# Splitting the first loads over two queues and moving two small loads back, at the head of a one-core attention and feed-forward kernel

## The chip, the cores and the metric

The kernel runs on one core of one Trainium2 chip. The metric is the device time of one execution in microseconds (us). One profiled execution of each kernel gives a trace; its span is about 1.7 us shorter than the device time. All times "at" a point are us from the span's start.

Engines: PE multiplies matrices, ACT and DVE work elementwise, POOL makes masks, SP only issues DMAs. ACT and POOL issue DMAs too, each on its own queue. POOL's queue is the software one (q0 in the profile), SP's and ACT's are hardware ones (q1 and q10).

## The reference

Two blocks of the same input x (2048 tokens, 512 features, bf16) are mixed by a gate for each token:

```python
g = sigmoid((x * gate_w).sum(-1, keepdims=True))
a = attention(x, wq, wk, wv, wo, beta)   # 32 heads of 16, in 4 segments of 512 tokens,
                                         # with a memory carried from segment to segment
b = ((relu(x @ W_gate)) * (x @ W_up)) @ W_down      # inner width 1792
return g * a + (1 - g) * b
```

Only the loads matter below: x (2 MB), wq, wk, wv (512 KB each), W_gate and W_up (1.8 MB each), and two tiny ones, beta (64 bytes, copied to all 128 partitions: the tile `betab`) and gate_w (1 KB, fetched as 512 separate 2-byte elements: the tile `gw`).

## The kernel before

The whole kernel is planned in Python: a list scheduler fixes the order of every engine's instructions beforehand. The chip then runs these fixed orders with semaphore waits. These are the loads at the head, in order of issue:

```python
    nc.gpsimd.dma_start(out=betab[:], in_=A_beta.partition_broadcast(P))
    with nc.allow_non_contiguous_dma(reason="1 KB"):
        nc.gpsimd.dma_start(out=gw[:], in_=gate_w.rearrange("(c p) -> p c", p=P))
    got_x0 = load(nc.sync, x0[:], x[0:L, :].rearrange("(t p) d -> p t d", p=P), L * D * 2)
    got_q = [load_cols(nc.scalar, wq_sb, A_wq, 0, D)] * 2
    got_k = [load_cols(nc.sync, wk_sb, A_wk, 0, D)] * 2
    got_v = load_cols(nc.scalar, wv_sb, A_wv, 0, D)
    # ... (cut) SP goes on: W_gate and W_up piece 0, then piece 1, then the transposing
    #     load of the second segment of x, then the other pieces, W_down, wo, more of x
```

`nc.sync` is SP, `nc.scalar` ACT, `nc.gpsimd` POOL. While these loads run, PE multiplies zeros to raise its clock; then it transposes segment 0 of x (x0), projects q, k and v, and goes on:

```python
    junk = sb([P, L], BF16, "junk")
    nc.vector.memset(junk[:], 0.0)          # after some other small memsets of DVE
    # ... (cut)
    for k in range(9):
        nc.tensor.matmul(wb[3][:], lhsT=junk[:, 0:P], rhs=junk[:], start=True, stop=True)
    order = plan.run()
    for t in order:
        if t.emit is not None:
            t.emit()
```

The softmax here doesn't subtract the row's maximum and nothing guards it: scores larger than these inputs give would overflow.

## Time and profile before

The time is 292.23 us (median of 3 runs, 292.07 to 292.28).

| What | Value | Where it is read |
|---|---|---|
| PE busy | 282.2 of 290.4 us, 97% | engine table |
| chain that ended last | 90% PE; largest single piece that is not PE: the DMA of wk | chain of waits |
| x0 landed, wq landed | 6.0 and 6.5 us | DMA issues: issue 0.81 plus 5.2 and 5.7 |
| q projections end, first wk matmul | 9.9 and 10.62 us | timeline |
| first large exponential | 14.47 us | timeline |

The piece of the chain of waits (start, length, what):

```profile
1.31 9.26 DMA wk_sb<-in_A_wk_dram
```

Four lines of the timeline (start, length, engine, line, operation, output and inputs, and in brackets how long the engine sat idle before and what ended that):

```profile
6.10 0.61 PE L315 MATMUL wb_133<-ident,E_83 128*128 128x128 bf16 x4 [0.22 <-DMA E_83<-in_A_x_dram]
...
8.88 1.02 PE L300 MATMUL wb_132<-xT,wq_sb 128*128 128x512 bf16 x4
10.62 1.04 PE L300 MATMUL wb_131<-xT,wk_sb 128*128 128x512 bf16 x4 [0.71 <-DMA wk_sb<-in_A_wk_dram]
...
14.47 1.88 ACT L455 ACTIVATE E_76<-sp 128x2048 bf16<-128x2048 f32 x1 [1.34 <-PE sp L434]
```

PE finished q and then waited 0.71 us for wk. From there on it is nearly always busy, so whatever makes wk land sooner moves everything.

Why wk took 9.26 us is in the windows view (busy time and instruction count of PE, PEld (PE's weight loads), DVE, ACT, POOL; the last three columns are PE's granted clock, the mean busy share of the DMA engines, and GB/s). Two columns need care. The clock column shows 1.00 wherever the trace has no record, and the first record here begins at 7.87 us. The DMA share counts every packet from its start to its end, so it exceeds 1 where packets overlap:

```profile
5.00:6.00 1.00, 0.88 (x3) 0.00 (x0) 0.00 (x0) 0.00 (x0) 1.00 (x2) 1.00 1.30 359
6.00:7.00 1.00, 0.90 (x9) 0.90 (x10) 0.25 (x1) 0.00 (x0) 0.44 (x2) 1.00 0.92 81
7.00:8.00 1.00, 1.00 (x11) 0.93 (x9) 0.57 (x2) 0.59 (x1) 0.00 (x0) 1.00 0.86 267
8.00:9.00 1.00, 0.97 (x5) 0.39 (x4) 0.03 (x1) 0.59 (x1) 0.00 (x0) 1.00 1.08 335
```

In 6 to 7 us the DMA engines are still busy for a share of 0.92, but move only 81 GB/s. The view of the DMA queues for 5 to 9 us says what held them (packets, MB, share of 16 engines' time):

```profile
q10 hardware_dynamic: 538, 0.53, 39.6%
q1 hardware_dynamic: 499, 0.50, 37.0%
q0 software_dynamic: 62, 0.01, 27.3%
```

The 62 packets of betab and gw took 27.3% of four microseconds of all sixteen engines, so 1.09 us of each engine, for 0.01 MB.

### The profile page before, as it was taken

Reading aid. Unit: us, or ns where it says so; the run is one execution under the profiler, and the core shown is the slowest. Engines: PE = TensorE matmul, PEld = TensorE weight load, DVE = VectorE, ACT = ScalarE, POOL = GpSimd, SP = SyncE. Lnnn points to the kernel's source line nnn. Section 1 sums busy time; section 2 is a strip of 40 time slices with the busy share of each in tenths; the row PEclk is TensorE's granted clock in tenths of the full one; section 3 lists DMA queues with packets and bytes.
Section 4 is the critical chain, followed back from the end, with each engine's and each line's share of the span. In section 5 each row is a group of like instructions: output and inputs, shape, how many; then the busy total and the mean of one; then the engine's idle time right before and its main releaser. Section 6 shows DMA issues by size and latency. Waiting matters only on the chain.

```text
span 290.4 us, 6923 instructions
## 1 busy us (share of the span) xinstructions
PE 282.2 (97%) x2905; PEld 138.5 (48%) x2905; DVE 176.5 (61%) x442; ACT 194.6 (67%) x168; POOL 88.5 (30%) x141
## 2 busy tenths in 40 slices
PE   7899999999999999999999999999999999999995
PEld 3344545454545353545353545346634545544442
DVE  1599896675946168569692558657947434554211
ACT  1289797789966678879866678787796767433100
POOL 7014443333242424342423243422324243200000
PEclk9999999999999999999999999999999999999999
DMA  6999962010110201100103010000100110010011
GB/s 178 341 277 344 187 121 43 2 21 18 29 29 21 56 18 20 20 18 2 36 2 76 20 36 3 19 2 2 20 18 3 36 38 27 12 20 0 0 36 36
DMA packets 32558, 15.91 MB, mean 55 GB/s; under 512 B 22016, under 2 KB 32528, under 8 KB 32528
## 3 DMA queue, kind: packets, MB, share of 16 engines
q1 hardware_dynamic: 31408, 14.42, 20.5%
q10 hardware_dynamic: 1056, 1.05, 1.1%
q8 instruction: 22, 0.36, 0.5%
q0 software_dynamic: 64, 0.01, 0.4%
q14 instruction: 8, 0.07, 0.1%
HBM read 8.14 MB, written 2.10 MB: 35 GB/s over the span
## 4 chain that ended last, share of the span: by engine, by line
PE 90%; ACT 3%; DMA 3%; DVE 1%; issue 0%; POOL 0%; SPq 0%; ACTq 0%
PE wb_131 L300 24%; PE wb_130 L300 21%; PE wb_133 L300 13%; PE wb_132 L300 10%; PE sp L434 9%; PE wb_132 L482 7%; DMA wk_sb<-in_A_wk_dram 3%; PE wb_130 L482 2%; PE wb_133 L482 1%; PE wb_133 L473 1%; ACT E_79 L455 1%; ACT E_78 L455 1%; ACT E_77 L455 1%; ACT E_76 L455 1%; PE wb_132 L542 1%; PE wb_133 L542 1%
## 5 line engine op out<-in xcount | busy, mean ns | idle before, releaser
L300 PEld LDWEIGHTS <-wu_sb 128*128 128x128 bf16 x224 | 20.2, 98 | 26.3 <-issue 4.9
L300 PEld LDWEIGHTS <-wg_sb 128*128 128x128 bf16 x224 | 19.9, 98 | 24.8 <-issue 4.5
L455 ACT ACTIVATE E_78<-sp 128x2048 bf16<-128x2048 f32 x10 | 18.8, 1877 | 7.0 <-PE sp L434 6.2
L300 PE MATMUL wb_130<-xT,wg_sb 128*128 128x512 bf16 x88 | 23.2, 380 | 0.0
L455 ACT ACTIVATE E_83<-sp 128x2048 bf16<-128x2048 f32 x10 | 18.8, 1876 | 6.3 <-PE sp L434 6.1
L455 ACT ACTIVATE E_79<-sp 128x2048 bf16<-128x2048 f32 x10 | 18.8, 1876 | 6.0 <-PE sp L434 6.0
L455 ACT ACTIVATE E_76<-sp 128x2048 bf16<-128x2048 f32 x10 | 18.8, 1877 | 5.5 <-PE sp L434 5.1
L455 ACT ACTIVATE E_82<-sp 128x2048 bf16<-128x2048 f32 x10 | 18.8, 1875 | 5.5 <-PE sp L434 4.5
L455 ACT ACTIVATE E_77<-sp 128x2048 bf16<-128x2048 f32 x10 | 18.8, 1876 | 5.4 <-PE sp L434 3.3
L455 ACT ACTIVATE E_80<-sp 128x2048 bf16<-128x2048 f32 x10 | 18.8, 1876 | 4.8 <-PE sp L434 4.0
L455 ACT ACTIVATE E_81<-sp 128x2048 bf16<-128x2048 f32 x10 | 18.8, 1876 | 4.2 <-PE sp L434 4.1
L300 PE MATMUL wb_133<-xT,wu_sb 128*128 128x512 bf16 x72 | 18.9, 380 | 0.0
L300 PE MATMUL wb_131<-xT,wu_sb 128*128 128x512 bf16 x72 | 18.7, 380 | 0.0
L461 POOL TENSOR_SCALAR_AFFINE_SELECT E_76<-E_76 128x512 bf16<-128x512 bf16 x16 | 10.3, 661 | 26.1 <-ACT E_76 L455 26.1
L461 POOL TENSOR_SCALAR_AFFINE_SELECT E_81<-E_81 128x512 bf16<-128x512 bf16 x16 | 11.7, 747 | 18.4 <-ACT E_81 L455 18.4
L461 POOL TENSOR_SCALAR_AFFINE_SELECT E_80<-E_80 128x512 bf16<-128x512 bf16 x16 | 10.9, 696 | 18.4 <-ACT E_80 L455 18.4
L461 POOL TENSOR_SCALAR_AFFINE_SELECT E_79<-E_79 128x512 bf16<-128x512 bf16 x16 | 10.2, 651 | 20.1 <-ACT E_79 L455 20.1
L461 POOL TENSOR_SCALAR_AFFINE_SELECT E_83<-E_83 128x512 bf16<-128x512 bf16 x16 | 10.0, 640 | 20.5 <-ACT E_83 L455 20.5
L461 POOL TENSOR_SCALAR_AFFINE_SELECT E_77<-E_77 128x512 bf16<-128x512 bf16 x16 | 10.3, 662 | 18.7 <-ACT E_77 L455 18.7
L461 POOL TENSOR_SCALAR_AFFINE_SELECT E_78<-E_78 128x512 bf16<-128x512 bf16 x16 | 9.9, 637 | 19.6 <-ACT E_78 L455 19.6
L461 POOL TENSOR_SCALAR_AFFINE_SELECT E_82<-E_82 128x512 bf16<-128x512 bf16 x16 | 10.0, 639 | 18.9 <-ACT E_82 L455 18.9
L576 ACT ACTIVATE rg<-wb_130 128x512 bf16<-128x512 f32 x22 | 13.1, 594 | 3.5 <-PE wb_130 L300 3.4
(541 smaller groups left out, 832.8 us busy)
## 6 DMA issues: line engine op xcount, KB each, us to landing
out_dram<-osb SPq DMA_DIRECT2D x16, 128.0 KB, 1.7
wd_sb<-in_B_W_down_dram SPq DMA_DIRECT2D x2, 896.0 KB, 10.4
wg_sb<-in_B_W_gate_dram SPq DMA_DIRECT2D x2, 512.0 KB, 11.5
wu_sb<-in_B_W_up_dram SPq DMA_DIRECT2D x2, 512.0 KB, 11.4
wg_sb<-in_B_W_gate_dram SPq DMA_DIRECT2D x2, 384.0 KB, 5.3
wu_sb<-in_B_W_up_dram SPq DMA_DIRECT2D x2, 384.0 KB, 6.6
wq_sb<-in_A_wq_dram ACTq DMA_DIRECT2D x1, 512.0 KB, 5.7
E_83<-in_A_x_dram SPq DMA_DIRECT2D x1, 512.0 KB, 5.2
```

The costliest lines, as they stand in the source:

```text
L300: nc.tensor.matmul(bank(sl), lhsT=lhsT, rhs=rhs, start=(start and q == 0), stop=(stop and q == n - 1))
L434: nc.tensor.matmul(sp[:, j, off:off + n], lhsT=kt[32 * j:32 * j + 32, kb * P:(kb + 1) * P], rhs=QT[i][32 * j:32 * j + 32, kb * P:kb * P + ...
L455: b = plan.add("ACT", 1880, key, lambda Ef=Ef: nc.scalar.activation(Ef[:], sp[:], ACT.Exp, scale=SCALE), [a] + eread.get(n - RE, []), ACL)
L461: nc.gpsimd.affine_select(out=m, in_=m, compare_op=ALU.is_ge, fill=0.0, base=0, pattern=[[0, 4], [1, P]], channel_multiplier=-1)
L473: nc.tensor.matmul(wb[sl.banks[1]][:, q2 * 136:(q2 + 1) * 136], lhsT=pqT[u % RQ][:, qb * P:(qb + 1) * P], rhs=mbd[i][:, c], start=(q2 == 0 ...
L482: nc.tensor.matmul(bank(sl)[:, lo:lo + HW], lhsT=E[(5 * u + f) % RE][:, j, o:o + P], rhs=Vp[i][:, kb, 8 * c + h8, 0:HW], start=(q2 == 0 an ...
L542: nc.tensor.matmul(wb[sl.banks[g // 2]][:, lo:lo + 136], lhsT=pK[i][:, t, g * P:(g + 1) * P], rhs=Vp[i][:, t, 8 * g:8 * g + 8, 0:HW], star ...
L576: nc.scalar.activation(rg[0][:], bank(sl), ACT.Relu)
```

## The change

The intent: x0 arrives sooner if both queues carry it first; the small loads get out of the way of the projection weights; PE's clock is warm when x0 arrives.

```diff
-    nc.gpsimd.dma_start(out=betab[:], in_=A_beta.partition_broadcast(P))
-    with nc.allow_non_contiguous_dma(reason="1 KB"):
-        nc.gpsimd.dma_start(out=gw[:], in_=gate_w.rearrange("(c p) -> p c", p=P))
-    got_x0 = load(nc.sync, x0[:], x[0:L, :].rearrange("(t p) d -> p t d", p=P), L * D * 2)
-    got_q = [load_cols(nc.scalar, wq_sb, A_wq, 0, D)] * 2
+    def load_halves(dst, src, k, nbytes):
+        src = src.rearrange("(c p) n -> p c n", p=P)
+        nc.sync.dma_start(out=dst[:, 0:k // 2], in_=src[:, 0:k // 2])
+        nc.scalar.dma_start(out=dst[:, k // 2:k], in_=src[:, k // 2:k])
+        return arrival(nbytes)
+
+    got_x0 = load_halves(x0, x[0:L, :], 4, L * D * 2)
+    got_q = [load_halves(wq_sb, A_wq, NC, D * D * 2)] * 2
     got_k = [load_cols(nc.sync, wk_sb, A_wk, 0, D)] * 2
     got_v = load_cols(nc.scalar, wv_sb, A_wv, 0, D)
+    nc.scalar.dma_start(out=betab[:], in_=A_beta.partition_broadcast(P))
+    with nc.allow_non_contiguous_dma(reason="1 KB"):
+        nc.scalar.dma_start(out=gw[:], in_=gate_w.rearrange("(c p) -> p c", p=P))
# ... (cut) the memset of junk moves ahead of DVE's and POOL's other memsets
-    for k in range(9):
+    for k in range(10):
         nc.tensor.matmul(wb[3][:], lhsT=junk[:, 0:P], rhs=junk[:], start=True, stop=True)
```

A constant of the scheduler also went from 3500 to 3300.

More of the change, by code (lines that the diff above doesn't have):

```diff
@@ L169 @@
     x0 = E[RE - 1]
-    clock = [3500.0]
+    clock = [3300.0]
     plan = Plan(4)
@@ L218 @@
     got_x[3] = [load_xT(3)]
+    junk = sb([P, L], BF16, "junk")
+    nc.vector.memset(junk[:], 0.0)
     ident = sb([P, P], BF16, "ident")
@@ L253 @@
     got_gates = plan.add("DVE", 900, 0.0, head_gates, [got_eb], 100)
-    junk = sb([P, L], BF16, "junk")
-    nc.vector.memset(junk[:], 0.0)
     sp = psum.tile([P, 4, L], F32, name="sp")
```

## The prediction

> **What bounds the kernel now.** The engine table gives PE 282.2 us busy of a 290.4 us span (97%), and the chain of waits is PE for 90%. Its one large piece that is not compute is at the head: the DMA of wk, issued at 1.31 us and landed 9.26 us later (3.2%). After it PE runs almost without a gap in a fixed order, so the question is when wk lets PE go on: by the timeline PE ends the second q projection near 9.9 us and waits until 10.62 us for wk. wv lands at 11.4 us and is used at 11.9 us.
>
> **Why wk lands so late.** The windows view shows the DMA rate: 387 and 359 GB/s in 4 to 6 us, then 81 in 6 to 7 us and 267 in 7 to 8 us, then about 346. The dip coincides with the software queue's packets: in 5 to 7 us the view of the DMA queues gives it 48% of all 16 engines for 19 packets and 0.01 MB. These are betab and gw, issued by POOL at 1.32 and 2.01 us and landing 7.0 and 7.9 us later. Against 350 GB/s the dip loses 0.35 MB, or 1.0 us, ahead of wk and wv.
>
> **The change.**
> 1. x0 and wq in halves. Today they land nearly together, at 6.0 and 6.5 us, because two queues share one rate (Trainium skill, "DMA: Bandwidth & Descriptors", section "Issuing engines are not separate DMA queues"; this trace agrees: 292 and 298 packets in 3 to 5 us). In halves x0 gets both shares: it is moved when 512 KB in all are, near 4.6 us by the windows, so landed near 4.9 us. wq stays near 6.3 us. The bytes ahead of wk do not change.
> 2. Small loads behind wv on ACT's queue. They leave the road in front of wk and wv: about 1.0 us, which is the gain. wk lands near 9.6 us, wv near 10.4 us. ACT issues five DMAs of about 0.5 us instead of two, so its table load ends near 4.9 us instead of 3.2, still before the first copy. betab lands near 11.5 to 12 us; its use moves to about 11.9 us, with a microsecond of slack before the first large exponential.
> 3. Ten matmuls on zeros from about 1.25 us instead of nine from 1.86. At 427 ns each they end near 5.5 us, sooner if the clock rises: transposes start there instead of at 6.10 us, and q ends near 9.0 us. This is hidden, as wk comes later.
>
> The order of the remaining instructions on every engine is unchanged.
>
> **On the critical path.** Only wk's landing: 10.57 to about 9.6 us. All that follows shifts whole by about 1.0 us: 291.2 us, with 290.5 to 291.9 us to hold it 8 times in 10. Chances: faster by over 2% 0.01, within 2% 0.98, slower 0.01.
>
> **What the profile would show.** Right: no dip at 6 to 8 us and no software queue; x0 landed by about 5 us, transposes near 5.5 us; the first wk matmul at 9.5 to 9.8 us, still released by the wk DMA; the first large exponential near 13.5 instead of 14.47 us, and the same 1 us at every later point. Wrong: the dip moves rather than disappears, or q instead of the wk DMA releases the wk matmuls.
>
> **What would make it wrong.** The small loads, issued in hardware, cost more engine time than now or slow wv; ACT stalls while issuing them and holds the xT copies; betab lands so late that it delays the first exponentials; or a later wait absorbs the microsecond.

## The result, and the profile after

The changed kernel takes 290.89 us (median of 4 runs, 290.83 to 290.92) against 292.25 us (4 runs) for the kernel before, 1.36 us less. The ratio is 0.9953, with a 95% interval from 0.9936 to 0.9970. Ratios are the mean time of one kernel's fast runs over that of the other's fast runs of the same rounds, so not quite the ratio of the medians quoted.

The piece of the chain of waits, after:

```profile
1.81 7.54 DMA wk_sb<-in_A_wk_dram
```

The timeline, after:

```profile
5.50 0.63 PE L321 MATMUL wb_135<-ident,E_83 128*128 128x128 bf16 x4
...
7.84 1.02 PE L306 MATMUL wb_134<-xT,wq_sb 128*128 128x512 bf16 x4
9.40 1.04 PE L306 MATMUL wb_133<-xT,wk_sb 128*128 128x512 bf16 x4 [0.54 <-DMA wk_sb<-in_A_wk_dram]
...
13.25 1.88 ACT L461 ACTIVATE E_76<-sp 128x2048 bf16<-128x2048 f32 x1 [1.34 <-PE sp L440]
```

wk lands at 9.35 us (1.81 + 7.54) instead of 10.57 us. Its first matmul is 1.22 us sooner, the first large exponential is 1.22 us sooner, and the last scaling of a result tile (DVE, 286.88 us before, 285.68 us after) is 1.20 us sooner. So the whole gain is made before 9.4 us and then carried to the end.

The windows view, after (columns as above):

```profile
6.00:7.00 1.00, 1.00 (x15) 0.84 (x13) 0.70 (x2) 0.63 (x3) 0.00 (x0) 1.00 0.98 313
7.00:8.00 1.00, 0.99 (x5) 0.38 (x4) 0.15 (x1) 0.57 (x2) 0.00 (x0) 1.00 1.07 368
8.00:9.00 1.00, 0.86 (x4) 0.19 (x2) 0.72 (x2) 0.00 (x0) 0.00 (x0) 1.00 1.06 358
9.00:10.00 1.00, 0.60 (x3) 0.31 (x4) 0.67 (x1) 0.00 (x0) 0.00 (x0) 1.00 0.53 154
10.00:11.00 1.00, 1.00 (x7) 0.47 (x5) 0.52 (x1) 0.00 (x0) 0.00 (x0) 1.00 0.95 280
```

The dip at 6 to 8 us is gone. A smaller one stands at 9 to 11 us, where the small loads now run. wk has landed by then, and nothing on the chain waits for what comes next.

One thing was not foreseen. ACT's fifth load (gw) was not issued at about 2.9 us: ACT waited until 4.4 us and issued it by 4.8 us, and the table load behind it ended at 6.13 us. From the timeline:

```profile
2.37 0.55 ACTq L203 DMA_DIRECT2D betab<-in_A_beta_dram  x1
...
4.44 0.38 ACTq L205 DMA_DIRECT2D gw<-in_gate_w_dram  x1
...
4.85 1.28 ACT L326 ACT_TABLE_LOAD   x1 [4.85 <-DMA E_83<-in_A_x_dram]
```

The last bracket names the cause: ACT waited for a half of x0 to land. The semaphores in the trace say why. The program counts the landings on both hardware queues with eight semaphores (counters that a load raises as it lands). From the ninth load on, each load first waits for the landing of the earlier load whose semaphore it takes over. gw took that of ACT's half of x0 (landed at 4.42 us), and SP's next piece of W_up that of the other half (landed at 4.09 us, piece issued at 4.11 us). So this wait belongs to the program, and every extra load on a hardware queue, a half or a small one, brings it sooner.

It did no harm here: ACT's first copy of transposed x started at 6.50 us, just as its input was ready.

### The profile page after: what moved, and what is told of

The parts are those of the page before. It is cut to its first block, busy times and chain, and to the rows that moved or that the text cites. A ratio compares the mean times of both kernels' runs of the same rounds, so it can differ in the third digit from the quotient of the medians.

```text
span 289.2 us, 6881 instructions
## 1 busy us (share of the span) xinstructions
PE 277.7 (96%) x2860; PEld 138.3 (48%) x2906; DVE 176.5 (61%) x442; ACT 194.5 (67%) x168; POOL 87.3 (30%) x139
## 4 chain that ended last, share of the span: by engine, by line
PE 88%; ACT 3%; DMA 3%; issue 2%; another core or an unknown queue 1%; DVE 1%; SPq 0%; POOL 0%; ACTq 0%
PE wb_133 L306 24%; PE wb_132 L306 20%; PE wb_135 L306 13%; PE sp L440 9%; PE wb_134 L306 8%; PE wb_134 L488 7%; DMA wk_sb<-in_A_wk_dram 3%; PE wb_132 L488 2%; PE wb_135 L488 1%; PE wb_135 L479 1%; ACT E_78 L461 1%; ACT E_76 L461 1%; ACT E_79 L461 1%; ACT E_77 L461 1%
## 5 line engine op out<-in xcount | busy, mean ns | idle before, releaser
L306 PE MATMUL wb_135<-xT,wu_sb 128*128 128x512 bf16 x68 | 18.5, 380 | 0.3 <-issue 0.2
L306 PE MATMUL wb_133<-xT,wu_sb 128*128 128x512 bf16 x68 | 18.5, 380 | 0.2
L467 POOL TENSOR_SCALAR_AFFINE_SELECT E_81<-E_81 128x512 bf16<-128x512 bf16 x16 | 11.7, 750 | 18.4 <-ACT E_81 L461 18.4
L467 POOL TENSOR_SCALAR_AFFINE_SELECT E_80<-E_80 128x512 bf16<-128x512 bf16 x16 | 10.9, 699 | 18.4 <-ACT E_80 L461 18.4
```

The costliest lines, as they stand in the source:

```text
L306: nc.tensor.matmul(bank(sl), lhsT=lhsT, rhs=rhs, start=(start and q == 0), stop=(stop and q == n - 1))
L467: nc.gpsimd.affine_select(out=m, in_=m, compare_op=ALU.is_ge, fill=0.0, base=0, pattern=[[0, 4], [1, P]], channel_multiplier=-1)
```

## The experiments

The theory after the result: wk's landing sets the time, and the small loads on POOL's queue were what delayed it. Rivals: the halves did it (A), or the earlier zeros did it (B). Three jobs of four kernels were run, five rounds each. The kernel before was at 292.21, 292.21 and 292.13 us (median) in them. "First wk matmul" and "first exponential" are from the profiled run. All twelve kernels gave correct results.

Some of these runs have a mean granted clock of 0.992 to 0.994 and lie 1.0 to 1.6 us above the median of their kernel. The profiled runs of e3 and e4 are two of them, and so are two of the eleven runs of the kernel before in the second job (293.74 and 293.64 us). The last two columns for e3 and e4 are therefore not typical of those kernels; those for g1 come from its fastest run.

| Kernel | Median us (range) | Ratio to before (95%) | First wk matmul, us | First exponential, us |
|---|---|---|---|---|
| before | 292.25 (292.07 to 292.41) | 1 | 10.62 | 14.47 |
| changed | 290.89 (290.83 to 290.92) | 0.9953 (0.9936 to 0.9970) | 9.40 | 13.25 |
| e1: small loads alone | 290.40 (290.26 to 290.84) | 0.9941 (0.9929 to 0.9953) | 8.97 | 12.82 |
| e2: halves alone | 292.19 (291.92 to 293.70) | 1.0006 (0.9988 to 1.0023) | 10.52 | 14.74 |
| e3: zeros alone | 292.36 (292.17 to 293.94) | 1.0012 (0.9997 to 1.0028) | 11.04 | 16.30 |
| e4: changed, small loads on POOL | 292.35 (292.10 to 293.32) | 1.0011 (0.9999 to 1.0023) | 10.20 | 15.72 |
| e5: betab alone moved | 292.10 (291.88 to 292.29) | 0.9992 (0.9976 to 1.0008) | 10.40 | 14.25 |
| f1: changed, halves undone | 290.31 (290.19 to 290.48) | 0.9930 (0.9915 to 0.9945) | 9.06 | 12.90 |
| f2: four loads in halves | 291.61 (291.28 to 291.94) | 0.9974 (0.9958 to 0.9990) | 8.36 | 12.20 |
| f3: f2 with seven zeros | 291.85 (291.22 to 293.21) | 0.9992 (0.9968 to 1.0016) | 7.93 | 12.28 |
| g1: f2, x segment 1 sooner | 290.07 (289.28 to 290.38) | 0.9925 (0.9913 to 0.9937) | 7.65 | 11.49 |
| g2: f3, x segment 1 sooner | 289.82 (289.74 to 289.92) | 0.9919 (0.9906 to 0.9931) | 7.31 | 12.03 |
| g3: f1, x segment 1 sooner | 290.47 (290.30 to 290.59) | 0.9940 (0.9928 to 0.9952) | 9.02 | 12.87 |
| g4: small loads twice on POOL | 292.92 (292.68 to 294.19) | 1.0039 (1.0021 to 1.0057) | 11.49 | 15.34 |

### e1: the small loads alone

```diff
-    nc.gpsimd.dma_start(out=betab[:], ...)      # and gw, at the front
     got_v = load_cols(nc.scalar, wv_sb, A_wv, 0, D)
+    nc.scalar.dma_start(out=betab[:], ...)      # and gw
```

> The kernel before with one part of the change: betab and gw moved from POOL's queue to ACT's queue behind wv. Theory (the software queue's packets cost the 16 engines about 1 us in front of wk): the dip at 6 to 8 us goes, wk releases PE near 9.6 to 9.8 us instead of 10.62, and the time falls by 0.8 to 1.1 us. Rival A (the halves do it): wk at 10.5 us and no change of time. Rival B (the earlier matmuls on zeros do it): no change either.

Measured: 290.40 us, 1.81 us less than before; the first exponential is 1.65 us sooner. Both rivals predicted no change, and both fall. The gain is also larger than the theory said, and larger than that of the whole change. From e1's timeline:

```profile
6.82 2.11 PE L300 MATMUL wb<-xT,wq_sb 128*128 128x512 bf16 x8
...
8.97 1.47 PE L300 MATMUL wb<-xT,wk_sb 128*128 128x512 bf16 x6
```

q ends at 8.93 us and wk lands near 8.9 us (issue 1.32 plus 7.6): PE hardly waits for wk any more.

One question e1 leaves open. It takes the two loads off the software queue and also moves them behind wk and wv; no run puts them on a hardware queue in front of wk, or on POOL's queue behind it. They are not free on ACT's queue either: in 9 to 11 us e1 moves 232 GB/s, so by an estimate 0.24 MB less than at 350 GB/s. There the packet records show 640 packets of 9 to 10 ns, 0.37 us of each engine in all, against 1.08 us for the two loads on POOL's queue. How much of the 1.81 us belongs to the queue and how much to the place in the order is not shown. (e1 also delays the second piece of W_gate, from 3.09 to 6.39 us, because the small loads now take two of the eight semaphores. In e2, e4 and e5 a second piece is delayed too, to 4.58, 4.49 and 6.43 us, without a gain.)

### e2: the halves alone

```diff
-    got_x0 = load(nc.sync, x0[:], ...)
-    got_q = [load_cols(nc.scalar, wq_sb, A_wq, 0, D)] * 2
+    got_x0 = load_halves(x0, x[0:L, :], 4, L * D * 2)
+    got_q = [load_halves(wq_sb, A_wq, NC, D * D * 2)] * 2
```

> The kernel before with x0 and wq in halves on the two queues; betab and gw stay on POOL. Theory: x0 lands near 4.5 us instead of 6.0, but the dip stays and wk, which is what releases PE, comes within 0.3 us of 10.6 us; time lower by 0 to 0.4 us (the start-up rate in 3 to 4 us, 213 GB/s before and 376 after, may belong to the halves and would then give up to 0.45 us). Rival A: nearly the whole gain of 1.36 us, wk near 9.4 us.

Measured: ratio 1.0006, no change, at the low end of what was expected. x0 did come sooner (PE began its transposes at 5.22 instead of 6.10 us), but PE then waited for the second half of wq, for wk and for wv.

### e3: the zeros alone

```diff
+    junk = sb([P, L], BF16, "junk")          # moved ahead of the other memsets
+    nc.vector.memset(junk[:], 0.0)
-    for k in range(9):
+    for k in range(10):
```

> The kernel before with only the memset moved up and ten matmuls on zeros instead of nine. Theory: x0 at 6.0 us and wk at 10.6 us are unchanged, so the time is unchanged within 0.1 us. Rival B: a higher clock from about 5 us on shortens what PE does and the time falls by some tenths.

Measured: ratio 1.0012, 0.15 us more than before, so no gain (rival B falls). The surprise is in the profiled run, which took 293.94 us, the longest of six. The windows view of that run:

```profile
9.00:10.00 1.00, 0.00 (x0) 0.00 (x0) 0.69 (x1) 0.00 (x0) 0.00 (x0) 1.00 1.10 339
10.00:11.00 1.00, 0.00 (x0) 0.00 (x0) 0.00 (x0) 0.00 (x0) 0.00 (x0) 1.00 1.09 346
11.00:12.00 1.00, 0.96 (x3) 0.41 (x4) 0.00 (x0) 0.00 (x0) 0.00 (x0) 0.63 1.10 348
12.00:13.00 1.00, 1.00 (x4) 0.32 (x3) 0.21 (x1) 0.00 (x0) 0.00 (x0) 0.50 1.11 351
```

The wait for wk there is 2.10 us instead of 0.71. The clock record of the trace then falls from 1.00 to 0.50 at 11.26 us and stays there for 3.41 us (0.63 is the mean of a window):

```profile
11.04 2.56 PE L300 MATMUL wb<-xT,wk_sb 128*128 128x512 bf16 x6 [2.10 <-DMA wk_sb<-in_A_wk_dram]
```

Six matmuls took 2.56 us; they took 1.47 us in e1. So in this run, to finish early and then idle was not free. The other five runs of e3 (292.17 to 292.49 us, mean clock 0.997 or more) show no such loss; how long PE waited in them is not recorded.

### e4: the changed kernel with the small loads back on POOL

```diff
+    nc.gpsimd.dma_start(out=betab[:], ...)      # and gw, at the front
-    nc.scalar.dma_start(out=betab[:], ...)      # and gw, behind wv
```

> The changed kernel with one part undone: betab and gw back on POOL's queue at the front. Theory: the dip returns at 5.5 to 8 us, wk releases PE about 1 us later than in the changed kernel (10.2 to 10.6 us against 9.40), time 291.8 to 292.2 us, so nearly the whole gain is lost. Rivals A and B: it keeps the gain, time near 290.9 us.

Measured: 292.35 us, ratio 1.0011, just above the range that the theory gave. The whole gain is gone, and with it rivals A and B. In its profiled run (293.32 us, again the longest of six) PE waited 2.12 us for wk, and the granted clock fell to 0.50 at 11.44 us, as in e3 (0.72 is the mean of 11 to 12 us):

```profile
11.00:12.00 1.00, 0.76 (x4) 0.10 (x1) 0.69 (x1) 0.01 (x1) 0.00 (x0) 0.72 1.11 352
...
10.20 1.56 PE L306 MATMUL wb<-xT,wk_sb 128*128 128x512 bf16 x6 [2.12 <-DMA wk_sb<-in_A_wk_dram]
```

### e5: only betab moved

```diff
-    nc.gpsimd.dma_start(out=betab[:], ...)      # gw stays on POOL, at the front
     got_v = load_cols(nc.scalar, wv_sb, A_wv, 0, D)
+    nc.scalar.dma_start(out=betab[:], ...)
```

> The kernel before with only betab moved behind wv; gw stays on POOL's queue. In the trace of before betab's packets are the long ones (0.6 to 1.2 us each, one per DMA engine), gw's take some 0.04 to 0.3 us. Theory: betab is the load that costs, so at least 80% of the gain of moving both (1.81 us) is there: 290.4 to 290.8 us. Rival (gw, the strided 2-byte load, costs as much): 291.3 us or more.

Measured: 292.10 us, ratio 0.9992. The theory (betab is the one that costs) falls. The rival's number holds, but not its reason: the two costs do not add up. Almost nothing is gained when one of the two loads stays. The queue view of e5 for 5 to 9 us:

```profile
q0 software_dynamic: 32, 0.00, 18.4%
```

gw alone takes 18.4% of four microseconds (0.74 us of each engine), where the two together took 27.3% (1.09 us). In the packet records of the trace, gw's sixteen 64-byte packets average 0.73 us here, against 0.11 us in the kernel before, where betab's came first (0.97 us). The hardware queues' 1 KB packets take 0.046 us. So the cost isn't betab's own: in these two kernels the load that came first on this queue had the long packets, whichever it was.

### f1: the changed kernel with the halves undone

```diff
-    got_x0 = load_halves(x0, x[0:L, :], 4, L * D * 2)
-    got_q = [load_halves(wq_sb, A_wq, NC, D * D * 2)] * 2
+    got_x0 = load(nc.sync, x0[:], ...)
+    got_q = [load_cols(nc.scalar, wq_sb, A_wq, 0, D)] * 2
```

> The changed kernel with the halves undone: x0 whole on SP's queue, wq whole on ACT's; small loads behind wv and the ten earlier matmuls on zeros stay. Theory after the first runs (the halves take back part of the gain, because wk is now the third load of SP's queue and is issued at 1.81 instead of 1.31 us): wk near 8.9 us and a time of 290.3 to 290.5 us, as with the small loads moved alone. Rival (the earlier zeros take it back): time stays near 290.9 us.

Measured: 290.31 us, as the theory said. All six runs (290.19 to 290.48) lie below all four of the changed kernel (290.83 to 290.92). They were not runs of the same job, and the intervals of the ratios touch, but the traces say the same: wk's first matmul at 9.06 us against 9.40, with or without the earlier zeros (e1: 8.97). So, in the changed kernel, the halves take back 0.3 to 0.6 us of the gain. f1's line:

```profile
9.06 1.46 PE L300 MATMUL wb<-xT,wk_sb 128*128 128x512 bf16 x6
```

How they do it can be read from the windows view. Up to 6 us the changed kernel moves more: 243, 376, 379 and 319 GB/s in the windows from 2 to 6 us, 1.32 MB, against 1.19 MB in e1 (196, 267, 380, 351). But summed from 2 us to the moment wk lands, e1 has moved 2.23 MB in all (8.91 us) and the changed kernel 2.43 MB (9.35 us). So 0.20 MB more of other loads' bytes go ahead of the last of wk, worth 0.6 us at 350 GB/s. The view of the queues puts them on SP's own queue (1.39 MB against 1.19 MB in e1; ACT's queue moved 1.05 and 1.04 MB), so they belong to loads that stand behind wk there. That wk's issue moves from 1.31 to 1.81 us does not explain it alone: f2 below issues wk's halves at 1.82 and 1.86 us and uses them at 8.36 us. Why the packets fall so is open.

### f2 and f3: all four loads in halves, small loads behind them on SP

Both are edits of the changed kernel.

```diff
-    got_k = [load_cols(nc.sync, wk_sb, A_wk, 0, D)] * 2
-    got_v = load_cols(nc.scalar, wv_sb, A_wv, 0, D)
-    nc.scalar.dma_start(out=betab[:], ...)      # and gw
+    got_k = [load_halves(wk_sb, A_wk, NC, D * D * 2)] * 2
+    got_v = load_halves(wv_sb, A_wv, NC, D * D * 2)
+    nc.sync.dma_start(out=betab[:], ...)        # and gw
# f3 also: range(10) -> range(7)
```

> A try at a better version: x0, wq, wk and wv all in halves on both queues, betab and gw on SP's queue behind wv so that ACT is free sooner, ten zeros. Theory (PE is released by wk's landing, and a load split over both queues gets both shares of the rate): wk lands near 7.9 us, so q's end near 8.6 us is what remains; time 290.0 to 290.4 us. If wk still lands at 9 us or later, splitting doesn't order the loads and the time is 290.7 us or more.

> The same with seven zeros instead of ten, so that PE takes x0 when it lands (about 4.5 us) instead of at 5.5 us. Theory: q ends near 7.9 us, wk is there near 7.9 us, wv near 9.3 us; time 289.2 to 289.8 us. Risk: fewer zeros leave PE's clock low for longer, and wk lands later than hoped; then 290.3 us or more.

Measured: 291.61 and 291.85 us, worse than hoped and worse than the changed kernel. Yet f2's head did what was asked: wk's matmuls began at 8.36 us, and the first exponential came 2.27 us sooner than before. From the fourth exponential on only 1.03 us are left. f2's timeline shows why:

```profile
19.32 1.04 PE L306 MATMUL wb<-xT,wq_sb 128*128 128x512 bf16 x3 [1.17 <-DMA xT<-in_A_x_dram]
```

PE now reaches the second segment of x before it has landed and waits 1.17 us. In f3 the same wait is 1.72 us, and f3 also waits 0.33 us within wk's matmuls. The semaphores have a part in this: the load of that segment takes over the one of the second half of wv, so it was issued at 10.01 us and landed at 19.28 us (8.72 and 18.69 us in the kernel before).

### g1, g2 and g3: the second segment of x ahead of the second pieces of the weights

```diff
     load_gu(0)
+    nc.sync.dma_start_transpose(out=xT[:, :, L:2 * L], in_=x[L:2 * L, :])
     load_gu(1)
-    got_x[1] = [load_xT(1)]
+    got_x[1] = [arrival(L * D * 2 * 1.3)]
```

The bookkeeping stays where it was, so the planned order of PE is the same. g1 is f2 with this edit, g2 is f3 with it, g3 is f1 with it.

> The try with all four loads in halves and ten zeros, with one edit: the transposing load of the second segment of x goes ahead of the second pieces of W_gate and W_up. In the try without it the first large exponential was 2.27 us sooner than in the kernel before, but PE then waited 1.17 us at 18.1 us for that segment and only 1.03 us were left. Theory (the later wait took the gain): the wait goes, all later points stay 2.2 us ahead, time 289.9 to 290.1 us. Rival (the loss has another cause): 291 us or more.

> The same edit with seven zeros instead of ten. Theory: wk's landing, not q's end, decides there (8.87 us in the try without the edit), so time 289.9 to 290.2 us, no better than with ten. If the earlier transposes are worth something, 289.7 us or less; if the lower clock of fewer zeros costs, 290.4 us or more.

> A control: the same edit on the kernel with x0 and wq whole, small loads behind wv and ten zeros (290.31 us), which has no wait for the second segment of x. Theory: no change, 290.2 to 290.4 us. If the edit helps by itself, 290.1 us or less.

Measured: g1 290.07 us, g2 289.82 us, g3 290.47 us. The wait at 18 us is gone in g1 and g2, and the lead at the first exponential is kept to the end in all three (2.92 of 2.98 us in g1's profiled run, 2.44 us in g2). The control g3 gains nothing, since f1 had no such wait. g2 is just below its expected range and g3 just above its own, each by less than 0.1 us. g1 and g2 are the fastest kernels, 0.8% below the kernel before; which of them is faster isn't settled. g1's profiled run was its fastest (289.28 us; the other four 290.06 to 290.38). In it, ten zeros took 3.71 us, against 4.45 us in the changed kernel. PE's clock rose sooner there: its record begins at 4.09 us, against 6.23 us in the changed kernel, and from then on a matmul on zeros takes 0.22 instead of 0.43 us. So part of g1's lead in the table is luck of that run.

### g4: the small loads twice

```diff
     # betab and gw on POOL's queue as before, then
+    nc.gpsimd.dma_start(out=betab2[:], in_=A_beta.partition_broadcast(P))
+    with nc.allow_non_contiguous_dma(reason="1 KB"):
+        nc.gpsimd.dma_start(out=gw2[:], in_=gate_w.rearrange("(c p) -> p c", p=P))
```

> The kernel before with both small loads made twice on POOL's queue (the second pair to tiles that nobody reads). The run with betab moved alone, in which gw's packets took about 1 us each instead, says that the cost comes once, with the first packet of the software queue on each DMA engine. Theory: the second pair is nearly free, wk within 0.3 us of 10.6 us, time 292.2 to 292.5 us. Rival (each pair of loads costs its own microsecond): wk near 11.6 us, time 293.0 us or more.

Measured: 292.92 us, 0.79 us more than before, and the first exponential 0.87 us later. This is outside both numbers. It refutes the theory that only the first packets cost. (That theory put gw's packets in e5 at about 1 us each; their mean is 0.73 us.) The queue view for 5 to 9 us:

```profile
q0 software_dynamic: 97, 0.02, 35.1%
```

So the cost rises with the number of loads on this queue, but not in proportion. Taking both away gains 1.65 us at the first exponential, taking one away gains 0.22 us, and adding two more costs 0.87 us. Why a 64-byte packet of this queue can hold an engine for 0.7 us stays open; no run here takes it apart.

## Why the prediction was right or wrong

The time was right: 291.2 us predicted, 290.5 to 291.9 us as range, 290.89 us measured. The mechanism was right in its main step, but two of its terms were mis-sized in opposite directions, and their errors partly cancelled. So it is partly luck that the time came out so close.

- "Only wk's landing" is on the critical path, and all that follows shifts whole: right. The lead is 1.22 us at the first wk matmul (9.40 us, just before the 9.5 to 9.8 us predicted) and 1.20 us at the last result tile.
- The small loads as the gain: right (e1, e4). "About 1.0 us" was too small: alone they give 1.65 us in the trace and 1.81 us in time. The estimate counted the 0.35 MB missing in the dip. From the windows from 2 to 9 us, the kernel before moved 1.84 MB and e1 2.26 MB, so 0.42 MB were missing. And when wk landed, 2.38 MB had been moved since 2 us in the kernel before, against 2.23 MB in e1: 0.15 MB more of other loads had gone ahead of it. Together that is 0.57 MB, or by an estimate 1.6 us at 350 GB/s.
- "The bytes ahead of wk do not change": this step failed. In halves, x0 landed at 4.4 us (predicted 4.9), but 0.20 MB more had been moved when wk was complete, and 0.3 to 0.6 us of the gain were given back (f1). The halves were predicted neutral; in this kernel they cost.
- The zeros: ended near 5.5 us as predicted, and q ended at 8.86 us (9.0 predicted). The change meant PE's clock to be warm when x0 arrived, and it was not: x0 landed at 4.4 us, and the clock record begins at 6.23 us. "This is hidden" holds for the changed kernel. But the profiled runs of e3 and e4 show that the hidden part is not always harmless: where PE idled for 2.1 us, its clock fell afterwards. The Trainium skill, "TensorE: Matmul & The Clock Gate", section "What's actually happening", says that activity releases the throttle and idleness brings it back; these two traces agree: the granted clock fell to 0.50 at 11.26 and 11.44 us.
- "No dip at 6 to 8 us": right. The prediction named a dip that moves as a sign that it was wrong. A dip did move, to 9 to 11 us (154 and 280 GB/s), behind wk, where it cost nothing. The sign was badly chosen: what matters is which load stands behind the dip.
- "ACT issues five DMAs of about 0.5 us": wrong in its detail. It left out that the semaphores run out: the fifth waited 1.52 us for a half of x0 to land, and the table load ended at 6.13 instead of 4.9 us. It stayed off the critical path.
- betab was expected at 11.5 to 12 us and landed near 11.1 us (2.37 + 8.7), before its use at 11.70 us.

## What to carry to other kernels

Find the one load that releases the busiest engine for good, and then count everything that is moved before it is complete; here two loads of 9 KB together, on the software queue and in front, cost 1.81 us, more than half a megabyte at 350 GB/s (1.5 us, an estimate). Test the parts of a change one by one even when the sum is as predicted: here one part alone (e1), or with the zeros (f1), was better than the whole. And after speeding up a head, look at the next load in line: f2's lead of 2.27 us shrank to 1.03 us at the first wait that had been just met before, and one reordered load brought it back.

## What the Trainium skill lacked or had wrong

- "DMA: Bandwidth & Descriptors" gives about 1 us for the first byte on the software path. Here betab was issued at 1.32 us, its first packet in the trace started at 5.90 us, 4.6 us later, and it landed 7.0 us after its issue, beside two hardware queues at work. SP's first packet started 1.1 us after its issue.
- The same page says that an engine takes turns between queues packet by packet, but gives no time for which a small packet of the software queue can hold it while two hardware queues are at work: 62 packets with 0.01 MB took 27.3% of all sixteen engines' time in 5 to 9 us, single 64-byte packets averaged 0.73 us (e5), and moving them behind wv on a hardware queue gained 1.65 us at the first exponential (e1).
- Its section "Issuing engines are not separate DMA queues" is right about the shared rate, but does not say that splitting loads over two queues changes which bytes go first: counted from 2 us, wk was complete after 2.43 MB in all with x0 and wq in halves, and after 2.23 MB with them whole (e1).
- "TensorE: Matmul & The Clock Gate" ties the return of the throttle to an idle window of about 3.4 us. Here the clock fell after a wait of 2.10 us (e3) and one of 2.12 us (e4): in the 3.41 us before it fell PE had been busy for 1.31 and 1.28 us, so the window need not be idle throughout. After waits of 1.75 us (g4) and 1.68 us (e2) the clock stayed at 1.00.
